# Where a query tile's low part, a rarely taken branch and a step's rows stand in a fused attention, experts and FFN kernel

## The chip, the cores and the metric

One core of a Trainium2 chip runs the whole program. The metric is the device time of one execution in microseconds (us). The engines are TensorE (PE), VectorE (DVE), ScalarE (ACT), GpSimd (POOL) and SyncE (SP); each takes its instructions in the order of the program, and they meet only at semaphores.

## What is computed

```python
def _attn_ref(q, k, v):                     # 4 x 8 heads, 576 rows, 64 columns
    scores = scale * np.matmul(q, k.transpose(0, 1, 3, 2))
    kth = np.partition(scores, -top_k, axis=-1)[..., -top_k:-top_k + 1]   # top_k = 32
    scores = np.where(scores >= kth, scores, -1000000000.0)
    attn = np.exp(scores - np.max(scores, axis=-1, keepdims=True))
    return np.matmul(attn / (np.sum(attn, axis=-1, keepdims=True) + 1e-09), v)

def _moe_ref(x, modality_id, w_gate, modality_bias, w1, w2):   # 2304 x 512, 8 experts, 1024
    logits = x @ w_gate + modality_bias[modality_id]
    e_idx = np.argmax(logits, axis=1)
...
    for e in range(E):
        h = np.maximum(x[mask] @ w1[e], 0.0)
        out[mask] = gate_w[mask, None] * (h @ w2[e])

def _moe2_ref(x, w_in, w_out):              # 2304 x 512, 2048
    h = x @ w_in
    g = np.where(h >= 1, h, np.where(h <= -1, 0.0, (h + 1) ** 2 / 4))
    return g @ w_out
```

## The kernel before

**Attention.** A pair is two heads of one batch; there are 16, each with 9 units of 128 queries. Two units are a group (72 groups), two groups share one tile of scores, a quad. The loop over groups `g` is written as a software pipeline: in the body of `g` the engines do the top 32 of group `g` (`topk`), the masks and transposes of group `g - 1`, the product with the values of group `g - 2`, and the scores of group `g + 4`.

`topk` on VectorE works on folded rows. In an odd group it also folds the next quad: `big` (L212), `c` (L213) and `lit2` (L214), the last two being the maximum and the minimum of the halves of `big`. GpSimd computes `lit`, the smaller one of each pair of scores (L227, L233: sum minus maximum), for the next group, and in an odd group waits with it until VectorE has made `lit2`. VectorE then takes the eight largest of `lit2` (L251) and of `lit` (L253). GpSimd also makes the small `nm` (L256) and the copies `edge` and `top` (L240), and for each pair `kl` and `ql` (L179, L183), which are the parts of keys and queries that the rounded `kh` and `qh` leave out, and the normalized output rows `x` and `xtail` (L348, L353).

Each pair is prepared some groups ahead: `turn` transposes keys or queries on TensorE and evicts them twice on ScalarE (`kT` and `kh`, `qT` and `qh`); `krest` and `qrest` make `kl` and `ql`. `prep` enters these four into the list `later` for the groups `g - 2` to `g`, where `g` is always odd. In its group such a list is worked off in order, its first two entries ahead of ScalarE's exponentials, the others at the body's end. `xout`, which makes `x` and `xtail` of an earlier pair, is put first in the list of an odd group.

**Experts.** Tokens are sorted by expert into chunks of 256 rows. A step is one or two chunks of an expert; for each of 8 columns `f` of its 1024 hidden units there is a piece `up` (L1054 to L1057, then `hh` and `hl`) and a piece `down` (L1063 to L1065). All pieces stand in one list, and `M.go(n)` writes out the next `n`. Ahead of each piece, `prepare` loads the weights of later pieces and splits those two pieces ahead into a high part (ScalarE) and a low part. The first two steps (`EARLY`) run while the routing of the last tokens is still being worked out: after each stage of `route_steps` on VectorE one piece is written out. The third step takes its expert and rows from the routing's table `tab`. In the second step `rows(st.next)` loads the third step's rows, and three of the later columns end with a `turn` that transposes them.

**The branch.** The top 32 of folded rows can miss an entry. `redo` says whether that happened anywhere; if so, a branch (L605) repeats the attention of that pair and `replay` repeats the experts' pieces done so far. Each engine reads `redo` and branches by itself; behind the branch the first use of another engine's work waits until that engine is through too. In the profiled run the branch's body isn't entered. Behind it, `reload` reads the registers of all steps that have some on SP again.

Of the kernel before, what the change touches and what calls it, by code (L numbers as in the profile page):

```python
# [23 lines left out]
NFE = FE // 128  # L24
# [6 lines left out]
EARLY = 2  # L31
# [34 lines left out]
class Kernel:  # L66
# [32 lines left out]
    def attention(self, moe):  # L99
        nc, tc = self.nc, self.tc  # L100
        with ExitStack() as ctx:
# [35 lines left out]
            raw, kq, st, xr = {}, {}, {}, {}  # L137
# [228 lines left out]
            def at(g, f, *a):  # L366
                later.setdefault(max(g, 0), []).append((f, a))

            def odd(g):
                return g if g % 2 else g - 1  # L370

            def prep(j, g, *eng):

                at(g - 2, turn, j, "k")
                at(g - 2, krest, j, *eng)
                at(g - 1, turn, j, "q")
                at(g, qrest, j, *eng)

            load(0, nc.scalar)
            load_v(0, vtile(0))  # L380
            load(1)
            load_v(1, vtile(1))
            prep(0, 0, nc.vector)
            for g in range(4):
                for f, a in later.pop(g, []):
# [5 lines left out]
            for j in range(1, len(pairs)):  # L391
                g = odd((9 * j + 1) // 2 - AHEAD - 2)
                prep(j, g)
                if j + 1 < len(pairs):
                    at(g - 2, load, j + 1)
# [150 lines left out]
            M = self.moe  # L546
# [35 lines left out]
            check_sum()  # L582
            for _ in self.route_steps():
                M.go(1)
            M.go(max(2 * NFE + 3 - M.at, 0))
            M.flush()
            M.apart = False

# [462 lines left out]
    def up(self, p, wh, wl, xh, xl, high=True, low=True):  # L1051
        nc = self.nc
        for c in range(KC if high else 0):
            nc.tensor.matmul(p, wh[c], xh[:, c, :], start=c == 0, stop=False)  # L1054
            nc.tensor.matmul(p, wl[c], xh[:, c, :], start=False, stop=False)  # L1055
        for c in range(KC if low else 0):
            nc.tensor.matmul(p, wh[c], xl[:, c, :], start=False, stop=c == KC - 1)  # L1057
# [221 lines left out]
class Experts:  # L1279
# [188 lines left out]
    def up(self, st, f):  # L1468
        nc = self.nc
        halves = st.next.halves if st.next else 0  # L1470
        if f == 2:
            self.rows(st.next)
        h, l = self.spl1.pop(self.n1[st, f])
        n = st.halves * 128
        p = self.bank("h")[:, 0:n]
        self.kn.up(p, [h[:, c] for c in range(KC)], [l[:, c] for c in range(KC)], st.xh, st.xl)
        hh, hl = (self.wide.tile([128, 2 * CAP], F32R, name="h" + x, bufs=2)[:, 0:n] if st.wide else
                  self.wk.tile([128, CAP], F32R, name="h" + x) for x in "hl")
        self.act(p, hh, hl)
        st.h[f] = hh, hl  # L1480
        t = f - NFE + 1 + halves
        if 0 <= t < halves:
            self.turn(st.next, t)
        if f == NFE - 2 and st.next and st.next.mate:
            self.rows(st.next.mate)
        self.work(self.up, st, f)
# [237 lines left out]
```

## Time and profile before

| | |
|---|---|
| median of 3 runs | 1181.84 us (1181.74 to 1182.97) |
| profiled execution | 1180.52 us, span 1178.9 us |
| busy: PE, DVE, ACT, POOL | 1109.3, 810.2, 709.8, 556.2 us |
| granted TensorE clock, mean | 0.977 |

The span is what the profile shows, from the first instruction to the last; the execution's own time is 1.6 us longer. Roughly, the attention takes the first 490 us, the experts run to 750 us, and the last network takes the rest. A busy time is the time in which an engine had an instruction under way; for TensorE, whose matmuls are pipelined, it is modelled.

### The profile page before, as it was taken

Reading aid. Unit: us, or ns where it says so; the run is one execution under the profiler, and the core shown is the slowest. Engines: PE = TensorE matmul, PEld = TensorE weight load, DVE = VectorE, ACT = ScalarE, POOL = GpSimd, SP = SyncE. Lnnn points to the kernel's source line nnn. Section 1 sums busy time; section 2 is a strip of 40 time slices with the busy share of each in tenths; the row PEclk is TensorE's granted clock in tenths of the full one; section 3 lists DMA queues with packets and bytes.
Section 4 is the critical chain, followed back from the end, with each engine's and each line's share of the span. In section 5 each row is a group of like instructions: output and inputs, shape, how many; then the busy total and the mean of one; then the engine's idle time right before and its main releaser. Section 6 shows DMA issues by size and latency. Waiting matters only on the chain. (4 is left out here: it accounts for less than half of the span.)

```text
span 1178.9 us, 24601 instructions
## 1 busy us (share of the span) xinstructions
PE 1109.3 (94%) x8900; PEld 944.4 (80%) x8901; DVE 810.2 (69%) x2523; ACT 709.8 (60%) x1262; POOL 556.2 (47%) x662
## 2 busy tenths in 40 slices
PE   8999899999998997887999999899999999999998
PEld 5777787877887885776888787778899999999897
DVE  6999999999999999887568889487332222323222
ACT  5989998999899985744554455254333333333322
POOL 2776777677677767622324455032322223232222
PEclk8989998999999997998999999999999999999999
DMA  4235573021111003366766565231101001010000
GB/s 88 55 114 176 185 233 119 15 45 44 25 27 37 12 13 126 108 205 212 239 198 214 187 224 179 78 130 54 54 1 37 19 1 54 1 55 1 27 1 28
DMA packets 120842, 106.66 MB, mean 90 GB/s; under 512 B 64384, under 2 KB 88960, under 8 KB 120704
## 3 DMA queue, kind: packets, MB, share of 16 engines
q1 hardware_dynamic: 116320, 94.67, 25.9%
q0 software_dynamic: 2880, 9.44, 2.4%
q8 instruction: 73, 1.20, 0.4%
q10 hardware_dynamic: 1504, 0.82, 0.2%
q14 instruction: 65, 0.53, 0.1%
HBM read 70.30 MB, written 34.60 MB: 89 GB/s over the span
## 5 line engine op out<-in xcount | busy, mean ns | idle before, releaser
L1206 POOL TENSOR_TENSOR gl<-g,gh 128x384 fp32r<-128x384 f32 x96 | 97.2, 1012 | 316.5 <-ACT gh L1205 289.5
L1200 ACT ACTIVATE c<-c,half 128x384 f32<-128x384 f32 x96 | 59.2, 617 | 161.9 <-DVE c L1199 157.1
L306 PE MATMUL tp<-nhuge,w 128*128 128x128 bf16 x720 | 137.1, 227 | 20.8 <-ACT w L295 20.5
L304 PE MATMUL tp<-ident,e 128*128 128x128 f32 x720 | 151.4, 297 | 0.5 <-issue 0.5
L1199 DVE TENSOR_SCALAR c<-h 128x384 f32<-128x384 f32 x95 | 52.8, 556 | 142.5 <-PE h L1057 140.1
L1054 PE MATMUL h<-xh,wih 128*128 128x384 f32 x380 | 130.5, 343 | 5.3 <-DVEq L1110 3.0
L1055 PE MATMUL h<-xh,wil 128*128 128x384 f32 x380 | 129.8, 341 | 0.0
L304 PEld LDWEIGHTS tp<-ident,e 128*128 128x128 f32 x720 | 105.4, 146 | 30.1 <-issue 11.2
L270 DVE MAX8 m<-z 128x8 f32<-128x160 f32 x432 | 117.5, 314 | 0.0
L1365 POOL TENSOR_TENSOR w1l<-w1r,w1h 128x512 fp32r<-128x512 f32 x41 | 57.7, 1408 | 124.7 <-ACT w1h L1364 98.4
L227 POOL TENSOR_TENSOR lit<-s 128x576 int32<-128x576 int32 x66 | 93.4, 1415 | 48.4 <-DVE lit L214 48.4
L1065 PE MATMUL y<-woh,gl 128*128 128x512 f32 x288 | 114.4, 397 | 1.5 <-POOL gl L1206 1.5
L1063 PE MATMUL y<-woh,gh 128*128 128x512 f32 x288 | 112.5, 391 | 1.7 <-ACT yo L1236 0.9
L1203 DVE TENSOR_TENSOR g<-c,h 128x384 f32<-128x384 f32 x95 | 52.6, 554 | 89.2 <-ACT c L1200 89.2
L1064 PE MATMUL y<-wol,gh 128*128 128x512 f32 x288 | 113.7, 395 | 0.0
L311 ACT ACTIVATE a<-tp 128x640 f32<-128x640 f32 x144 | 102.0, 708 | 18.9 <-PE tp L306 14.9
L295 ACT ACTIVATE w<-s,m 128x576 bf16<-128x576 f32 x144 | 103.6, 772 | 13.9 <-DVE m L270 13.9
L323 PE MATMUL tp<-v,a 128*64 128x65 f32 x2880 | 104.7, 228 | 2.1 <-issue 2.0
L323 PEld LDWEIGHTS tp<-v,a 128*64 128x64 f32 x2880 | 93.8, 141 | 15.5 <-issue 8.3
L290 ACT ACTIVATE e<-s,nm 128x576 f32<-128x576 f32 x144 | 103.5, 771 | 4.3 <-POOL nm L256 4.2
L306 PEld LDWEIGHTS <-w 128*128 128x128 bf16 x720 | 79.2, 111 | 26.9 <-ACT w L295 26.5
L204 ACT ACTIVATE s<-sp 128x576 f32<-128x576 f32 x144 | 92.8, 648 | 10.7 <-PE sp L196 9.1
(313 smaller groups left out, 2938.6 us busy)
## 6 DMA issues: line engine op xcount, KB each, us to landing
w1r<-in_moe_w_dram SPq DMA_DIRECT2D x56, 256.0 KB
w2r<-in_moe_w_dram SPq DMA_DIRECT2D x56, 256.0 KB
xs_dr<-zero SPq DMA_DIRECT2D x19, 512.0 KB
ys_dr<-zero SPq DMA_DIRECT2D x19, 512.0 KB
cr<-in_moe_w_in_dram SPq DMA_DIRECT2D x16, 512.0 KB
cr<-in_moe_w_out_dram SPq DMA_DIRECT2D x16, 512.0 KB
rows<-xs_dr SPq DMA_DIRECT2D x20, 256.0 KB
ys_dr<-rows SPq DMA_DIRECT2D x17, 256.0 KB
```

The costliest lines, as they stand in the source:

```text
L270: nc.vector.max(m8[:, i, r + 1], z[:, i])
L290: nc.scalar.activation(e, s, AF.Exp, bias=nm, scale=0.125)
L295: nc.scalar.activation(w, s, AF.Relu, bias=t, scale=-1.0)
L304: nc.tensor.matmul(o, e[:, k0:k0 + 128], self.ident, is_transpose=True, start=True, stop=False)
L306: nc.tensor.matmul(o, w[:, k0:k0 + 128], self.nhuge, start=False, stop=True)
L311: nc.scalar.activation(a, p[:, 0:640], AF.Relu)
L323: nc.tensor.matmul(o[HS[i]], a[:, k0:k0 + 64], v_[:, u % 2 if u < 8 else i, kc, :], start=kc == 0, stop=kc == 4)
L1054: nc.tensor.matmul(p, wh[c], xh[:, c, :], start=c == 0, stop=False)
L1055: nc.tensor.matmul(p, wl[c], xh[:, c, :], start=False, stop=False)
L1063: nc.tensor.matmul(y[t], hh[:, o], wh, start=first, stop=False)
L1064: nc.tensor.matmul(y[t], hh[:, o], wl, start=False, stop=False)
L1065: nc.tensor.matmul(y[t], hl[:, o], wh, start=False, stop=last)
```

## The change

```diff
             def prep(j, g, *eng):
...
                 at(g - 2, turn, j, "k")
                 at(g - 2, krest, j, *eng)
-                at(g - 1, turn, j, "q")
-                at(g, qrest, j, *eng)
+                at(g - 2, turn, j, "q")
+                at(g - 1, qrest, j, *eng)
...
             for _ in self.route_steps():
                 M.go(1)
-            M.go(max(2 * NFE + 3 - M.at, 0))
+            M.go(max(2 * NFE + 5 - M.at, 0))
             M.flush()
...
     def up(self, st, f):
         nc = self.nc
         halves = st.next.halves if st.next else 0
-        if f == 2:
+        late = st.n == EARLY - 1
+        if f == 2 + late:
             self.rows(st.next)
...
-        t = f - NFE + 1 + halves
+        t = f - NFE + 1 + halves - late
         if 0 <= t < halves:
             self.turn(st.next, t)
```

For each pair, the queries' transposes go from the even group `g - 1` to the end of the odd group `g - 2`, and `ql` from the odd group `g` to the even group `g - 1`. Two more pieces are written out ahead of the branch, `up` of column 2 and `down` of column 1 of the second step. In the second step the next step's rows are loaded at column 3 instead of 2, and transposed at columns 5 to 7 instead of 4 to 6.

On GpSimd, around one pair in the attention, from the keys' low part to the end of the odd group two later, the order before is:

```order
L179 TENSOR_TENSOR kl<-kT,kh 128x576
L240 COPY edge<-c 128x4
L240 COPY top<-m_1276 128x2
L256 TENSOR_SCALAR nm<-m_1410 128x2
L227 TENSOR_TENSOR lit<-s_1004 128x576
L233 TENSOR_TENSOR lit<-lit,big 128x576
L240 COPY edge<-c 128x4
...
L348 TENSOR_TENSOR x_73<-xr,r 128x4x128
L353 TENSOR_TENSOR xtail_77<-xr,r 64x64 x2
L183 TENSOR_TENSOR ql_116<-qT,qh_115 128x512
L240 COPY edge<-c 128x4
```

And after the change:

```order
L179 TENSOR_TENSOR kl<-kT,kh 128x576
L240 COPY edge<-c 128x4
L240 COPY top<-m_1276 128x2
L256 TENSOR_SCALAR nm<-m_1419 128x2
L227 TENSOR_TENSOR lit<-s_1013 128x576
L233 TENSOR_TENSOR lit<-lit,big 128x576
L183 TENSOR_TENSOR ql_116<-qT,qh_115 128x512
L240 COPY edge<-c 128x4
...
L348 TENSOR_TENSOR x_73<-xr,r 128x4x128
L353 TENSOR_TENSOR xtail_77<-xr,r 64x64 x2
L240 COPY edge<-c 128x4
```

`ql` has left its place behind `x` and `xtail` and stands behind the `lit` of the even group before them.

On SP, ahead of the branch, from the last transfer of the second step's pieces to the reading of `redo` (`tab` is the routing's table, `w1r` and `w2r` are raw weights), before:

```order
L1335 DMA w1r<-in_moe_w_dram 128x4x128
L1438 ISA
L1438 DMA ys_dr<-rows 128x512
L605 TENSOR_LOAD redo
L605 ISA x2
L605 COMPARE_AND_BRANCH
```

And after the change (lines are 1 or 2 higher there):

```order
L1439 DMA ys_dr<-rows 128x512
L1340 ISA
L1340 DMA w2r<-in_moe_w_dram 128x512
L1322 TENSOR_LOAD tab
L1322 ISA x2
L1319 TENSOR_LOAD tab
L1319 ISA x2
L1319 TENSOR_LOAD tab
L1319 ISA x2
L1336 ISA
L1336 DMA w1r<-in_moe_w_dram 128x4x128
L606 TENSOR_LOAD redo
```

Two loads of weights now come ahead of the branch, the second of them the third step's first, and with it three reads of that step's entries in the table.

## Rows read from the trace of the kernel before

**Rows 1.** Windows: length, busy PE, PEld, DVE, ACT, POOL, PEclk, DMA share, GB/s.
```profile
217.97:256.26 38.29, 35.97 (x500) 29.81 (x501) 36.71 (x156) 37.59 (x68) 27.04 (x36) 1.00 0.11 25
...
sum 349.58, PE 328.57 PEld 273.98 DVE 331.43 ACT 320.38 POOL 255.46; mean PE 27.38 PEld 22.83 DVE 27.62 ACT 26.70 POOL 21.29
...
750.00:1179.00 429.00, 415.54 (x2084) 371.41 (x2082) 155.91 (x270) 151.99 (x265) 112.66 (x111) 1.00 0.11 36
```

**Rows 2.** Groups from 50 to 440 us: busy us, mean ns, idle before, releaser.
```profile
L253 DVE MAX8 c<-lit 128x8 f32<-128x288 f32 x120 | 48.4, 445 | 18.1 <-POOL lit L233 18.1
...
L183 POOL TENSOR_TENSOR ql<-qT,qh 128x512 fp32r<-128x512 f32 x13 | 16.6, 1278 | 1.0
```

**Rows 3.** Timeline of GpSimd in an odd group: start, duration, instruction, idle before.
```profile
134.96 1.28 POOL L183 TENSOR_TENSOR ql<-qT,qh 128x512 fp32r<-128x512 f32 x1
136.18 0.19 POOL L240 COPY edge<-c 128x4 f32<-128x4 f32 x1
...
138.13 1.42 POOL L233 TENSOR_TENSOR lit<-lit,big 128x576 int32<-128x576 int32 x1
```

**Rows 4.** Timeline of VectorE, behind those rows and one quad later.
```profile
137.74 0.50 DVE L251 MAX8 c<-lit 128x8 f32<-128x144 f32 x2
139.59 0.82 DVE L253 MAX8 c<-lit 128x8 f32<-128x288 f32 x2 [1.34 <-POOL lit L233]
...
151.76 0.80 DVE L253 MAX8 c<-lit 128x8 f32<-128x288 f32 x2
...
152.93 1.34 DVE L212 TENSOR_TENSOR big<-s 128x1152 f32<-128x1152 f32 x1
```

**Rows 5.** Timeline of GpSimd at the end of an even group.
```profile
151.40 0.19 POOL L240 COPY edge<-c 128x4 f32<-128x4 f32 x1
...
153.10 1.24 POOL L256 TENSOR_SCALAR nm<-m 128x2 f32<-128x2 f32 x1 [1.39 <-DVE m L255]
```

**Rows 6.** Timelines of ScalarE and GpSimd in two pairs' preparation.
```profile
144.40 0.65 ACT L204 ACTIVATE s<-sp 128x576 f32<-128x576 f32 x1
146.58 1.44 ACT L295 ACTIVATE w<-s,m 128x576 bf16<-128x576 f32 x2 [1.53 <-DVE m L270]
...
151.68 0.59 ACT L172 ACTIVATE qh<-sp 128x512 fp32r<-128x512 f32 x1
...
236.15 0.65 ACT L175 ACTIVATE kh<-sp 128x576 fp32r<-128x576 f32 x1
...
237.12 1.44 POOL L179 TENSOR_TENSOR kl<-kT,kh 128x576 fp32r<-128x576 f32 x1
```

**Rows 7.** Timeline of TensorE around the branch.
```profile
530.24 0.29 PE L1054 MATMUL h<-xh,w1h 128*128 128x256 f32 x1
...
532.84 0.39 PE L1065 MATMUL y<-w2h,hl 128*128 128x512 f32 x1
537.10 0.39 PE L1054 MATMUL h<-xh,w1h 128*128 128x256 f32 x1 [3.87 <-ACTq L605]
539.97 0.58 PE L1055 MATMUL h<-xh,w1l 128*128 128x256 f32 x1 [2.49 <-DVEq L605]
...
548.99 0.60 PE L1045 MATMUL pT<-ident,rows 128*128 128x128 f32 x4
```

**Rows 8.** Timeline of VectorE around the branch.
```profile
532.59 0.42 DVE L1466 SCALAR_TENSOR_TENSOR hl<-h,hh 128x256 fp32r<-128x256 f32 x1
...
534.20 0.68 DVE L1365 TENSOR_TENSOR w1l<-w1r,w1h 128x512 fp32r<-128x512 f32 x1
...
535.99 0.15 DVE L945 CAST nsi<-ns 128x1 int32<-128x1 f32 x1
540.19 0.31 DVE L950 TENSOR_TENSOR lg<-lg,mx 128x144 f32<-128x144 f32 x1 [4.05 <-DVEq L605]
```

**Rows 9.** Timeline of SP's transfers behind the branch.
```profile
542.53 0.36 SPq L1339 DMA_DIRECT2D w2r<-in_moe_w_dram  x1
544.93 0.33 SPq L1380 DMA_DIRECT2D rows<-xs_dr  x1
```

## The prediction

> **What bounds the kernel now.** I read the table of windows first, cut at the moments where VectorE had just waited in the attention, then the groups of VectorE and GpSimd over the attention, then the timelines of the two engines around one such moment, and last the timelines around the branch.
>
> Twelve periods of the attention (75 to 425 us) last 349.58 us, in which VectorE is busy for 331.43, TensorE 328.57, ScalarE 320.38, GpSimd 255.46 [rows 1]. VectorE is first by a little, and its idle time has one cause: its maximum over `lit` (line 253) waits for GpSimd 18.1 us in all between 50 and 440 us; in the same stretch GpSimd makes `ql` 13 times [rows 2]. One of these waits: in an odd group GpSimd does `lit` for this group, the output rows `x` and `xtail`, then `ql` from 134.96, the copies from 136.18, and only then the `lit` of the next group, which ends at 139.55 [rows 3]. VectorE was through with line 251 at 138.24 and starts line 253 at 139.59, after 1.34 us of waiting; a group later it starts it at 151.76 without a wait [rows 4]. So `ql` stands ahead of the very result for which VectorE stops. The last 429 us belong to TensorE, busy for 415.54 [rows 1]: what is won earlier is carried to the end.
>
> **The change, part by part.**
>
> Low part of the queries. From the start of `ql` to the next instruction GpSimd spends 136.18 - 134.96 = 1.22 us [rows 3]. Without it the next `lit` ends at 138.33 instead of 139.55, against 138.24 on VectorE: of the wait of 1.34 some 0.1 stays. Over 13 pairs: 13 x 1.22 = 15.9 us of the 18.1 are taken away, 2.2 stay. All of this is on the path, as VectorE has no other idle time there to speak of.
>
> Where `ql` goes. It now follows the `lit` of the even group, ready at 151.40, where the copies start today; after them GpSimd waits 1.39 us for VectorE [rows 5]. So `ql` would run from 151.40 to about 152.6 and the two copies to about 152.9. VectorE's next fold begins at 152.93 [rows 4]. It costs nothing, but with hardly 0.1 us to spare. Without this cover it costs its 1.22 us again.
>
> The queries' transposes and their two evictions on ScalarE (`qh` 0.59 us, `qT` about the same) move from the body of the even group to the end of the odd one. There ScalarE is through at 145.05 and then waits 1.53 us for VectorE [rows 6]: about 1.1 us of evictions fits. `ql` finds its inputs at about 146.2, five us before GpSimd comes to it. The pair's loads are issued where they were, and nothing of the move issues a transfer.
>
> Can the others follow? TensorE and ScalarE have 21 and 29 us of idle time in the twelve periods, where VectorE gives up 12 x 1.22 = 14.6 [rows 1]. On average they can. In the period from 217.97 ScalarE is busy for 37.59 of 38.29 us [rows 1] and can't shorten it by 1.22; it will trail VectorE, which needs its scores only two groups later. The tight place is the keys' low part: `kh` ends at 236.80 and `kl` starts at 237.12 [rows 6]. With VectorE and GpSimd 1.22 us earlier and ScalarE not, `kl` waits 0.9 us, and about that goes to VectorE. I take 0.9 off, once: 15.0 us. The bounds: half, 8, if ScalarE or TensorE turn out to set the pace over long stretches (their busy shares are 92 and 94%), and 18.1, all of the wait.
>
> The branch. TensorE ends its last piece at 533.23, passes the branch in 3.87 us, starts one matmul, and waits 2.49 more until VectorE is through too, at 539.97 [rows 7]. VectorE came late: its last routing step ends at 536.14 and its first work behind the branch is at 540.19, 4.05 us later [rows 8]. The pieces that now come first, `up` 2 and `down` 1 of the second step, are 530.24 to 533.07 in length, 2.84 us for a pair [rows 7]. TensorE would reach the branch at 536.1, while VectorE first does three more instructions (`hl` 0.42, two weight splits of 0.68 [rows 8], some 1.6 us with their overlap) and passes at 541.5 or so. TensorE resumes 1.55 us later with 2.84 us more done: a gain of 1.3. It would be 2.8 if VectorE's three were hidden.
>
> The table's registers. SP now reads three of the table's values ahead of the branch, because the load of the third step's first weights is pulled ahead of it, and reads them again behind it. Three such reads take 544.93 - 542.53 - 0.36 = 2.0 us [rows 9]. Ahead of the branch they start when the table is ready (about 536) and delay SP to about 538.4. Behind it, the load of `w2r` and the three loads of rows queued behind the reads come about 2 us later, at 547 for the first rows. Their first transpose, now one column later in the step, stands 1.55 us later too, at about 550.5 instead of 548.99 [rows 7]. Of the present distance (4.1 us from issue to transpose) about 0.6 is lost, and no wait is visible there today. The last transpose now has one `down` (1.4 us) less until the third step uses the columns; two evictions of about 0.6 us fit. I cost this part at nothing; its bound is 3 us, if each of the three transposes waits about one us. The branch as a whole lies between -2 and +2.8 us.
>
> The sum: 15.0 + 1.3 = 16.3 us from the profiled execution's 1180.52, so 1164.2. The median of the runs is 1181.84, 1.3 above it: 1165.5 us.
>
> **A rule against it.** The `nm` that GpSimd starts at 153.10 lasts 1.24 us, until 154.34, just behind the end of VectorE's `big` at 154.27 [rows 4, 5]: of two that meet, one stands still. The Trainium skill, SBUF — State Buffer, section "SBUF: two separate sides", says that VectorE with two operands in SBUF and GpSimd share a port pair as an exclusive lock: whoever starts first keeps it for the whole instruction. By that rule a `ql` that is still running when the fold begins holds VectorE; the trace agrees for the other direction, and no row here shows this one.
>
> **The rivals.**
> - The moved `ql` meets the fold. If it runs some tenths late, as little as 0.1 to 0.3 us, VectorE's fold or GpSimd's copies wait. At worst the 1.22 us are paid there 13 times, 15.9 us are given back, and the branch's 1.3 is left: 1180.5, no change. For it: the gap ends at 152.93 and `ql` with its copies at 152.9. Against: copies and `nm` in VectorE's way are short, and the next `lit` waits for the fold anyway.
> - ScalarE or TensorE set the pace and half comes back: 1181.84 - 8 - 1.3 = 1172.5. For it: 37.59 of 38.29 us. Against: the spare time of the neighbouring periods.
> - The attention gives what it should, and the rows or the weights come late behind the branch, for 3 to 4 us: 1169.
> - Slower: GpSimd works in order, so if `qh` comes after GpSimd has reached `ql`, copies, `nm` and the next `lit` stand behind it. Today's figures leave 5 us (2.3 us in the tight period). If ScalarE trails VectorE by more than that, each further us lands on VectorE; from 1.22 us on, some 6.5 us of lag, it is worse than before. At 0.4 us beyond, 13 x 0.4 = 5 us: 1187. Against: ScalarE has less work than VectorE over the twelve periods.
>
> **How the numbers follow.** The forecast, 1165.5, has a chance of 0.70, the pace of the others 0.12, late rows 0.06, the fold 0.05, the slower case 0.04, and a gain above 18 us with a faster TensorE 0.03. The low end is all of the wait and all of the branch: 1181.84 - 18.1 - 2.8 = 1161. The high end takes in half of the attention's gain and a lost branch, 1174. Outside lie the fold, the slower case and the larger gain, 0.12, and the tails of the others: under 0.2 in all. A measurement of this kernel tells 0.2%, 2.4 us, from no change. Faster 0.91, the same 0.05, slower 0.04.
>
> **What would show it.** `ql` right behind the even group's second `lit`; line 253's waits for GpSimd down from 18.1 to 2 or 3 us, with no new wait at line 212; the attention's end 15 us earlier; the distance from TensorE's last matmul ahead of the branch to its second behind it down from 6.7 to about 5.4 us; the third step's transposes without a wait for their rows. Wrong would be: the waits at line 253 at the same sum, VectorE waiting for ScalarE's `s` or at line 212, or `kl` starting later than the `lit` ahead of it ends, in most pairs.

## The result, and the profile after

The changed kernel needs 1169.81 us in the median (1167.26 to 1177.03, 4 runs) where the kernel before needed 1182.40 beside it: ratio 0.9899, interval 0.9868 to 0.9930. A second reading, beside other kernels below, gave 0.9915 (0.9896 to 0.9934). By these numbers 10 to 12.6 us are gained. The forecast was 16.3 us and 1165.5. The profiled execution took 1170.9 us, with a span of 1169.3.

The windows again, first the same twelve periods of the attention (they answer to [rows 1]; length, busy PE, PEld, DVE, ACT, POOL, PEclk, DMA share, GB/s), then the end of the program.

```profile
74.33:411.99 337.66, 322.22 (x4169) 271.04 (x4166) 331.72 (x1401) 317.38 (x565) 256.50 (x331) 0.98 0.28 83
...
741.00:1169.00 428.00, 415.11 (x2083) 371.41 (x2081) 155.85 (x270) 151.88 (x265) 112.80 (x111) 1.00 0.11 36
```

VectorE has the same work, 331.7 us, in 337.66 instead of 349.58 us: its idle time went from 18.2 to 5.9. A period is 28.14 us long instead of 29.13. What lies ahead of them won another 0.95 (74.33 against 75.28), so that VectorE stands at line 253 at 411.99 where it stood at 424.86, 12.87 us earlier. The groups from 50 to 440 us show the same (busy us, mean ns, idle before, releaser; for [rows 2]):

```profile
L253 DVE MAX8 c<-lit 128x8 f32<-128x288 f32 x122 | 49.2, 445 | 4.7 <-POOL lit L233 4.1
...
L179 POOL TENSOR_TENSOR kl<-kT,kh 128x576 fp32r<-128x576 f32 x13 | 18.4, 1419 | 4.1 <-ACT kh L175 4.1
...
L183 POOL TENSOR_TENSOR ql<-qT,qh 128x512 fp32r<-128x512 f32 x13 | 16.7, 1283 | 0.0
```

Line 253 waits 4.1 us instead of 18.1. New against that profile is that `kl` waits for `kh`; in `branch_only` below, whose attention is the one before, it does so once, for 2.18 us. Now the timelines of GpSimd and VectorE at the end of an even group, the new place of `ql` (for [rows 4, 5]):

```profile
146.65 1.42 POOL L233 TENSOR_TENSOR lit<-lit,big 128x576 int32<-128x576 int32 x1
148.03 1.28 POOL L183 TENSOR_TENSOR ql<-qT,qh 128x512 fp32r<-128x512 f32 x1
149.25 0.18 POOL L240 COPY edge<-c 128x4 f32<-128x4 f32 x1
149.38 0.18 POOL L240 COPY top<-m 128x2 f32<-128x2 f32 x1
...
148.35 0.80 DVE L253 MAX8 c<-lit 128x8 f32<-128x288 f32 x2
...
149.52 1.34 DVE L212 TENSOR_TENSOR big<-s 128x1152 f32<-128x1152 f32 x1
```

`ql` ends at 149.31, its two copies at 149.56, and VectorE's fold starts at 149.52, without a wait and with its old length. In this pair that is the prediction's margin, to the tenth. In four of the 13 pairs between 50 and 440 us the fold begins 0.01 to 0.02 us ahead of `ql`'s end and takes 1.35 to 1.37 us, so there is nothing to spare. The waits that are left at line 253 are nine up to 411.99: seven of 0.19 to 0.30, and the two shown here, with the `kl` that stands ahead of each in GpSimd's timeline:

```profile
231.71 1.42 POOL L179 TENSOR_TENSOR kl<-kT,kh 128x576 fp32r<-128x576 f32 x1 [1.62 <-ACT kh L175]
...
307.83 1.42 POOL L179 TENSOR_TENSOR kl<-kT,kh 128x576 fp32r<-128x576 f32 x1 [1.84 <-ACT kh L175]
...
236.49 0.82 DVE L253 MAX8 c<-lit 128x8 f32<-128x288 f32 x2 [1.18 <-POOL lit L233]
...
312.57 0.82 DVE L253 MAX8 c<-lit 128x8 f32<-128x288 f32 x2 [1.37 <-POOL lit L233]
```

GpSimd stands 1.62 and 1.84 us at `kl`; five us later its `lit` is late for VectorE by 1.18 and 1.37.

At the branch, the timelines of TensorE, VectorE and of SP's transfers (for [rows 7 to 9]; line 606 is the branch):

```profile
523.35 0.39 PE L1066 MATMUL y<-w2h,hl 128*128 128x512 f32 x1
526.42 0.36 PE L1055 MATMUL h<-xh,w1h 128*128 128x256 f32 x1 [2.69 <-PEq L606]
527.50 0.52 PE L1056 MATMUL h<-xh,w1l 128*128 128x256 f32 x1 [0.72 <-DVEq L606]
...
538.84 0.66 PE L1046 MATMUL pT<-ident,rows 128*128 128x128 f32 x4 [2.61 <-DMA rows<-xs_dr]
...
524.59 0.68 DVE L1366 TENSOR_TENSOR w1l<-w1r,w1h 128x512 fp32r<-128x512 f32 x1
527.72 0.31 DVE L951 TENSOR_TENSOR lg<-lg,mx 128x144 f32<-128x144 f32 x1 [2.45 <-DVEq L606]
...
525.44 0.38 SPq L1336 DMA_DIRECT2D w1r<-in_moe_w_dram  x1
534.39 0.35 SPq L1340 DMA_DIRECT2D w2r<-in_moe_w_dram  x1
535.09 1.47 SPq L1381 DMA_DIRECT2D rows<-xs_dr  x3
```

From TensorE's last matmul ahead of the branch to its second one behind it there are 527.50 - 523.74 = 3.76 us; before there were 539.97 - 533.23 = 6.74. So the branch itself won 2.98 us. Eleven us on, the first transpose of the third step stands 2.61 us for its rows.

### The profile page after: what moved, and what is told of

The parts are those of the page before. It is cut to its first block, busy times and chain, and to the rows that moved or that the text cites. A ratio compares the mean times of both kernels' runs of the same rounds, so it can differ in the third digit from the quotient of the medians.

```text
span 1169.3 us, 24602 instructions
## 1 busy us (share of the span) xinstructions
PE 1106.4 (95%) x8900; PEld 944.4 (81%) x8901; DVE 807.9 (69%) x2524; ACT 708.7 (61%) x1262; POOL 553.9 (47%) x661
## 3 DMA queue, kind: packets, MB, share of 16 engines
q8 instruction: 74, 1.21, 0.4%
## 5 line engine op out<-in xcount | busy, mean ns | idle before, releaser
L304 PE MATMUL tp<-ident,e 128*128 128x128 f32 x720 | 144.8, 292 | 2.4 <-ACT e L290 2.4
L306 PE MATMUL tp<-nhuge,w 128*128 128x128 bf16 x720 | 133.2, 224 | 6.2 <-ACT w L295 5.1
L1366 POOL TENSOR_TENSOR w1l<-w1r,w1h 128x512 fp32r<-128x512 f32 x40 | 54.0, 1350 | 134.8 <-ACT w1h L1365 85.6
L311 ACT ACTIVATE a<-tp 128x640 f32<-128x640 f32 x144 | 102.3, 710 | 19.6 <-PE tp L306 15.2
L233 POOL TENSOR_TENSOR lit<-lit,big 128x576 int32<-128x576 int32 x66 | 93.5, 1417 | 5.2
```

What stands on the lines that cost most here:

```text
L304: nc.tensor.matmul(o, e[:, k0:k0 + 128], self.ident, is_transpose=True, start=True, stop=False)
L306: nc.tensor.matmul(o, w[:, k0:k0 + 128], self.nhuge, start=False, stop=True)
L311: nc.scalar.activation(a, p[:, 0:640], AF.Relu)
```

## The experiments

All kernels here were timed beside the kernel before, on the same chip; a ratio is to that kernel. They ran in three groups, each on another chip: `attn_only`, `branch_only`, `defer_load` and `rows_ahead`; `ql_twice`, `q_rest_only`, `k_first` and `defer_k_first`; and the other four. From one profile to the next the unchanged parts move by some us (below), so trace positions are compared over short distances and totals by ratios.

### The two parts apart

`attn_only` has the queries' part alone, `branch_only` the rest. Their edits against the changed kernel:

```diff
# attn_only
-            M.go(max(2 * NFE + 5 - M.at, 0))
+            M.go(max(2 * NFE + 3 - M.at, 0))
...
-        late = st.n == EARLY - 1
+        late = 0
# branch_only
-                at(g - 2, turn, j, "q")
-                at(g - 1, qrest, j, *eng)
+                at(g - 1, turn, j, "q")
+                at(g, qrest, j, *eng)
```

> Only the queries' part of the change; the branch and the third step's rows stand where they stood before. Theory A (the later branch wins some 2.8 us at the branch and gives them back until the FFN, because the rows and weights behind it come late): the attention's 12.9 us are all that the change was worth, so this kernel needs 1182.4 - 12.9 = 1169.5 us, no more than the changed kernel, and the third step's first transpose has no wait for its rows. Rival B (the later branch keeps its gain of 1.3 to 2.8 us, and the loss lies in the stages behind it whatever the branch does): 1169.8 + 1.3 to 1169.8 + 2.8, so 1171.1 to 1172.6 us.

> Only the branch two pieces later and the third step's rows one column later; the queries' part as before. Theory A: nothing is left of the gain at the branch, 1182.4 us within 1.5, with the wait of about 2.6 us for the rows at the third step's first transpose. Rival B (and the prediction's own term): 1.3 to 2.8 us faster, 1181.1 to 1179.6.

Measured: `attn_only` 0.9896 (0.9872 to 0.9920), `branch_only` 1.0007 (0.9987 to 1.0028). The queries' part alone is as good as the whole change, and of the branch's part no gain shows, within some 0.3%. The totals favour theory A but don't prove it: `attn_only`'s interval takes in the times of both theories, and `branch_only`'s still takes in, at its edge, a gain of 1.3 us (0.9989). In `attn_only` the third step's first transpose (535.77) has no wait, as theory A said. TensorE in `branch_only`, whose profiled execution (1190.22 us) was 5 us above its median:

```profile
544.55 0.55 PE L1055 MATMUL h<-xh,w1h 128*128 128x256 f32 x1 [2.75 <-PEq L606]
545.55 0.58 PE L1056 MATMUL h<-xh,w1l 128*128 128x256 f32 x1 [0.45 <-DVEq L606]
...
556.09 0.66 PE L1046 MATMUL pT<-ident,rows 128*128 128x128 f32 x4 [1.03 <-DMA rows<-xs_dr]
...
565.97 0.44 PE L1055 MATMUL h<-xh,w1h 128*128 128x384 f32 x1
```

The last row is the third step's first `up`. From the branch's second matmul to there it takes 20.42 us; in the kernel before 560.34 - 539.97 = 20.37, though there one more pair of pieces (2.84 us) lies between. So 2.89 us are given back in this stretch, against 2.98 won. Only 1.03 of them is the wait for rows; 0.67 is a wait for VectorE's `hl`. The rest has no row of its own (TensorE's clock stood at 0.50 for 5.1 us of this stretch, and for 4.4 before).

The other profiles say the same. From the end of VectorE's last routing step, `nsi`, to the third step's first `up` there are 24.2 us in the kernel before, 24.9 in `attn_only` and 24.2 in `attn_k_first` (below), which have its branch; in the seven profiles with the branch of the change, here and below, there are 24.2 to 25.3. What is won at the branch is gone at the third step in every one.

### What makes the rows late

Three ways to bring them earlier. `defer_load` holds the third step's first load, and with it the three table reads, until the branch is passed; `one_piece` passes the branch one piece later than before instead of two, where that load isn't due yet; `rows_ahead` issues the rows behind the branch ahead of everything but their three reads.

```diff
# defer_load, in load1; the held loads are issued after M.reload()
+            if self.hold is not None and st.e is None and st.n >= EARLY:
+                self.hold.append(k)
+                return
...
# one_piece
-            M.go(max(2 * NFE + 5 - M.at, 0))
+            M.go(max(2 * NFE + 4 - M.at, 0))
# rows_ahead
-            M.reload()
...
-        if f == 2 + late:
+        if f == 2 and not late:
...
+        one = self.steps[EARLY]
+        if one.e is not None:
+            self.regs(one)
+        self.rows(one)
+        for st in self.steps[:EARLY]:
+            self.regs(st)
```

> The changed kernel, but the load of the third step's first weights, with the three table reads that SyncE makes for it, is held back until SyncE is behind the branch. Theory 1 (the reads ahead of the branch keep SyncE at the branch and so make the rows late): SyncE passes the branch about 2 us earlier, the first rows are issued near 533 instead of 535.1, the wait of 2.61 us at the first transpose shrinks to 0.5 or so, and the kernel needs 1167 to 1168 us against 1169.8. Rival 2 (SyncE passes the branch when TensorE and VectorE do, and what makes the rows late is the seven reads and the weight load that stand ahead of them behind the branch, now one load more): the wait stays at 2.6 us or grows by 0.7, and the time stays at 1169.8 within 1.

> The changed kernel, but the branch comes one piece later than before instead of two. The load of the third step's first weights, with the table reads, then stands behind the branch by itself. If the table reads ahead of the branch are what makes the rows late, the wait for the rows at the third step's first transpose is 0.75 us or less, as in the run that holds this load back (2.61 in the changed kernel), and the third step's first up comes 1 to 2 us earlier against the last routing step. If it is the time from the branch to the rows' issue, whatever is read ahead, the wait is 2 us or more. Of the total 0 to 2 us below the changed kernel, which the interval hardly tells.

> The changed kernel, but behind the branch SyncE reads the third step's three registers first, then issues the three loads of rows, and only then reads the two early steps' four registers and loads w2r. Theory 1 and rival 2 of the run that holds the weight load back both say that the rows come some 3 us earlier and the wait of 2.61 us at the first transpose goes. Theory A goes on: as the rows were the loss, the kernel gains 2 to 2.6 us, 1167.2 to 1167.8. Rival C (w2r, now about 2 us later, is late next: ScalarE's w2h waits for it already, 2.71 us): TensorE waits for the second weights instead, and the time stays at 1169.8 within 1.

Measured: 0.9901 (0.9876 to 0.9925), 0.9903 (0.9875 to 0.9931) and 0.9900 (0.9878 to 0.9922). In the totals none differs from the changed kernel. The first transposes of `defer_load`, `one_piece` and `rows_ahead`:

```profile
537.70 0.66 PE L1048 MATMUL pT<-ident,rows 128*128 128x128 f32 x4 [0.75 <-DMA rows<-xs_dr]
```

```profile
543.27 0.60 PE L1046 MATMUL pT<-ident,rows 128*128 128x128 f32 x4
```

```profile
539.58 0.60 PE L1045 MATMUL pT<-ident,rows 128*128 128x128 f32 x4
...
544.78 0.66 PE L1045 MATMUL pT<-ident,rows 128*128 128x128 f32 x4 [1.62 <-DVE xl L1049]
...
542.43 0.63 ACT L1365 ACTIVATE w2h<-w2r 128x512 fp32r<-128x512 f32 x1 [4.58 <-DMA w2r<-in_moe_w_dram]
```

The wait for rows is not the same in each execution: in the seven profiles with the branch of the change it is 1.03 (`branch_only`) to 2.61 us, 2.16 in the changed kernel's second one. With the load held back it is 0.75, and nothing in `defer_k_first` (below); in `one_piece`, where TensorE also has a piece more to do ahead of the transposes, it is nothing too. So theory 1 holds for the wait: SP's reading of `redo` starts 2.1 us behind the end of the last routing step in the changed kernel, where it starts 3.0 us ahead of it in `defer_load` and `one_piece`, and 3.6 ahead in the kernel before. In `defer_load` the stretch from the end of VectorE's last routing step (524.44) to the third step's first `up` (546.20) is 21.76 us, where the changed kernel takes 24.36, from 523.72 to 548.08: 2.6 us less. In `defer_k_first` it is 22.4. So up to this point most of what the branch won is kept. The totals don't show it: the expected 1167 to 1168 us (0.987 to 0.988) lie at the lower edge of `defer_load`'s interval or below. In `rows_ahead` the rows come in time, but `w2r` is issued 10.9 us behind SP's last load ahead of the branch (528.79 to 539.71) instead of 8.95, ScalarE waits 4.58 us for it, VectorE's `w2l` and `xl` slip, and TensorE waits 1.62 us for `xl` at the second transposes instead: rival C. The rows were the first of several things that are late behind the branch.

### What the cover of `ql` is worth

`ql_twice` computes `ql` twice in a row; `q_rest_only` leaves the queries' transposes in the even group.

```diff
# ql_twice, in qrest
-                eng.tensor_tensor(lo, t[:, 0:512], hi.bitcast(F32), op=ALU.subtract)
+                for i in range(2):
+                    eng.tensor_tensor(lo, t[:, 0:512], hi.bitcast(F32), op=ALU.subtract)
# q_rest_only, in prep
-                at(g - 2, turn, j, "q")
+                at(g - 1, turn, j, "q")
```

> The changed kernel with ql computed twice in a row, at its new place behind the even group's second lit (same inputs, same output). It asks what the cover at the new place is worth: the first ql ends where VectorE's fold begins (237.62 against 237.68 in the changed kernel), so the second one runs into the fold. Theory 1 (the prediction's rival: of a ql and a fold that meet one stands still, and VectorE pays): the fold starts some 1.2 us later in 13 pairs, 1169.8 + 15.6, so about 1185 us, with idle time at lines 212 or 213 or a longer fold. Rival 2 (VectorE goes on; GpSimd, which waits 1.33 us for the fold's end before its next lit, takes the 1.2 us out of that wait): VectorE's waits at line 253 stay near 4 us and the time stays at 1169.8 within 2.

> The changed kernel, but the queries' transposes with qT and qh stay in the even group where they were, ahead of ql in the same group. ScalarE makes kh some 1.5 us after GpSimd is free for kl in the odd group; qh would come 2 to 3 us after GpSimd has reached ql in the even one. Theory 1 (the prediction's slower rival: copies, nm and the next lit stand behind a ql that waits, and what goes beyond the 1.33 us that GpSimd has to spare lands on VectorE): 13 times 0.3 to 1.4 us, so 1174 to 1188 us, with waits at line 253 or for the scores. Rival 2 (the wait takes the place of the one for the fold, and the lit of the odd group is needed only some 0.8 us after it is ready): within 2 us of 1169.8.

`ql_twice`: 1.0073 (1.0054 to 1.0091), some 20 us slower than the changed kernel and 8 slower than the kernel before. GpSimd and VectorE at one of its even groups, VectorE at another (212.11), and the fold's group from 50 to 440 us (line 213 there):

```profile
248.68 2.65 POOL L184 TENSOR_TENSOR ql<-qT,qh 128x512 fp32r<-128x512 f32 x2
...
250.19 2.35 DVE L213 TENSOR_TENSOR big<-s 128x1152 f32<-128x1152 f32 x1
...
212.11 1.34 DVE L213 TENSOR_TENSOR big<-s 128x1152 f32<-128x1152 f32 x1
213.48 1.72 DVE L214 TENSOR_TENSOR c<-big 128x576 f32<-128x576 f32 x1
...
L213 DVE TENSOR_TENSOR big<-s 128x1152 f32<-128x1152 f32 x30 | 50.3, 1677 | 0.0
```

The fold starts at 250.19, while the second `ql` runs until 251.33. It ends at 252.54, 1.21 us behind `ql`'s end where it needs 1.34 alone, and is recorded as 2.35 us of work, not as a wait. Ten of the 30 folds take 2.32 to 2.38 us, and all of them 50.3 instead of 30 x 1.343 = 40.3. In three pairs, such as that at 212.11, the fold starts first, by 0.1 us: then it keeps its 1.34 us, the second `ql` takes 2.4, and the next fold step stands instead (1.72 us). Line 254 (253 elsewhere) adds 4.1 us of waits, and the next fold step (0.855 instead of 0.760 us in the mean) 2.8. The named parts make 16.9 of the 20 us, and one more wait at line 254 ahead of 50 us another 2.8. Theory 1 holds, at more than its price. This is the rule that the prediction weighed (the Trainium skill, SBUF — State Buffer, section "SBUF: two separate sides": whoever starts first keeps the shared port for its whole instruction). The trace agrees: the fold advances only when `ql` is through, within 0.13 us, and where the fold is first it is `ql` that stands. So these two engines meet elsewhere than at semaphores, too.

`q_rest_only`: 0.9920 (0.9902 to 0.9938). GpSimd's `ql` from 50 to 440 us, VectorE's two long waits, and one `ql` with its fold:

```profile
L183 POOL TENSOR_TENSOR ql<-qT,qh 128x512 fp32r<-128x512 f32 x13 | 16.6, 1279 | 15.0 <-ACT qh L172 15.0
```

```profile
208.75 0.82 DVE L253 MAX8 c<-lit 128x8 f32<-128x288 f32 x2 [2.54 <-POOL lit L233]
...
325.13 0.82 DVE L253 MAX8 c<-lit 128x8 f32<-128x288 f32 x2 [2.68 <-POOL lit L233]
```

```profile
239.17 1.28 POOL L183 TENSOR_TENSOR ql<-qT,qh 128x512 fp32r<-128x512 f32 x1 [1.23 <-ACT qh L172]
...
239.39 2.27 DVE L212 TENSOR_TENSOR big<-s 128x1152 f32<-128x1152 f32 x1
```

GpSimd stands 15.0 us for `qh`, in five of the 13 pairs; in the other eight `qh` is in time. Twice it stands over 6 us, and VectorE waits 2.54 and 2.68 us for `lit`. Three times it stands 0.38 to 1.23 us, which puts `ql` into the fold, and VectorE pays as in `ql_twice`: the folds take 2.27, 1.85 and 1.42 us instead of 1.34, and one more ahead of 50 us takes 2.17. So theory 1 describes the pairs in which `qh` is late, by two ways that cost 5.2 and 2.3 us. Its attention ends at 477.79, 4.9 us later than the changed kernel's, of which the waits at line 253 make 2.7 and the folds 2.3; the ratios put the whole kernel 0.5 to 2.5 us behind the changed one. So the earlier transposes matter, and `ql` behind the even group's `lit` is worth having without them.

### Where the attention's last two us are

`k_first` puts the keys' transposes, `kT`, `kh` and `kl` ahead of the transposes and evictions `a` of the weights in the odd group. `defer_k_first` adds `defer_load`. Behind them came the changed kernel and `k_first` once more, side by side, and `attn_k_first`: the queries' part and the keys first, with the branch as before.

```diff
                     scores(g + AHEAD, 0)
+                if bg and bg[0][0] is turn and bg[0][1][1] == "k":
+                    for f, a in bg[:2]:
+                        f(*a)
+                    bg = [(id, (0,))] * 2 + bg[2:]
```

> The changed kernel, but in the odd group the keys' transposes, kT, kh and kl stand ahead of the transposes of the weights and their evictions a, which take ScalarE 1.46 us. Theory 1 (the attention gave 12.9 instead of 15.0 to 15.9 us because kl waited for kh, 6.9 us in five pairs, and VectorE lost 1.18 and 1.37 us by it): kl no longer waits, line 253's waits for GpSimd fall from 4.1 to about 1.5 us, the attention ends 2.5 us earlier, 1167.3 us. Rival 2 (ScalarE has no spare time in these periods; what kh gains, a and e lose, and the wait turns up at the scores or at the next nm): line 253 may fall, but VectorE's last line 253 stays at about 473 and the time at 1169.8 or above.

> Both mends together: the keys ahead of the weights' evictions as in the run before this one, and the third step's first weight load with its table reads held back behind the branch. If both theories hold, 2.5 us in the attention and 2.3 us between the branch and the third step's first rows: 1169.8 - 4.8 = 1165.0 us. If only the held load helps 1167.5; if neither, 1169.8.

> The changed kernel itself once more, beside the others of this job, so that differences of a few us between them can be read on one chip. Its ratio was 0.9899; if the reading repeats, 0.989 to 0.992. In its first profile the granted clock stood at 0.50 from 468 to 476 us, where the run with the keys first had 1.00; theory 1 (that level differs from execution to execution, whatever the kernel) says that the clock of this stretch is another one here.

> The kernel with the keys first once more. It came out 16.4 us faster than the kernel before, though its attention ended no earlier than the changed kernel's (472.7 against 472.9), and its lead showed only behind it, where the granted clock stood at 1.00 instead of 0.50. Theory 1 (the lead was the clock of these executions and the other chip): the ratio is that of the changed kernel beside it within 0.2%. Rival 2 (the order of ScalarE's work with the keys first keeps TensorE busier before the end of the attention, and the clock stays up more often): 0.3 to 0.4% below the changed kernel again, 0.986, with the clock at 1.00 between 468 and 480.

> The queries' part and the keys first, with the branch and the third step's rows where they were in the kernel before. If the later branch is worth nothing (its run alone gave 1.0007), this kernel equals the one with the keys first and the later branch, within 0.2%. If it is worth the prediction's 1.3 us or the 2.9 us that it wins at the branch itself, this kernel is 0.1 to 0.25% slower than that one.

Measured, with the sum of the waits above 0.5 us at line 253 up to 440 us, and how much earlier than before (485.79) VectorE's last line 253 stands. The last three rows are kernels of the sections above, whose attention is the changed kernel's:

| kernel | ratio, interval | long waits, us | earlier by, us | both, us |
|---|---|---|---|---|
| changed | 0.9899 (0.9868 to 0.9930) | 2.55 | 12.89 | 15.44 |
| after_again | 0.9915 (0.9896 to 0.9934) | 2.57 | 13.14 | 15.71 |
| attn_only | 0.9896 (0.9872 to 0.9920) | 1.83 | 13.35 | 15.18 |
| k_first | 0.9858 (0.9841 to 0.9875) | 1.79 | 13.08 | 14.87 |
| k_first_again | 0.9894 (0.9874 to 0.9914) | 1.06 | 14.76 | 15.82 |
| attn_k_first | 0.9876 (0.9851 to 0.9901) | 0 | 15.36 | 15.36 |
| defer_k_first | 0.9855 (0.9834 to 0.9876) | 2.31 | 13.16 | 15.47 |
| defer_load | 0.9901 (0.9876 to 0.9925) | 3.39 | 11.73 | 15.12 |
| rows_ahead | 0.9900 (0.9878 to 0.9922) | 6.24 | 9.12 | 15.36 |
| one_piece | 0.9903 (0.9875 to 0.9931) | 4.72 | 8.42 | 13.14 |

`attn_k_first` has none of these waits, and GpSimd's `kl` none for `kh` (groups of its attention):

```profile
L253 DVE MAX8 c<-lit 128x8 f32<-128x288 f32 x122 | 49.3, 446 | 2.1 <-POOL lit L233 1.5
```

```profile
L179 POOL TENSOR_TENSOR kl<-kT,kh 128x576 fp32r<-128x576 f32 x13 | 18.5, 1420 | 0.0
```

The last column is 15.4 within 0.6 in nine of the ten. In `one_piece` 2.2 us more are lost ahead of 60 us, in two of VectorE's instructions for the routing (1.53 and 1.42 us instead of 0.42 and 0.32). So the move of `ql` is worth some 15.4 us, and what `kl` loses by `kh` comes off it about one for one. The keys first don't reliably cure it: how many pairs wait, and which, differs between executions of one kernel. Still, the four profiles with the keys first lose 0 to 2.3 us by these waits, the six without 1.8 to 6.2, and all four ratios (0.9855 to 0.9894) lie below the six (0.9896 to 0.9915). Side by side the intervals overlap (0.9894 against 0.9915), so a gain of some 3 us is likely, and not shown. `attn_k_first`, without the later branch, is no slower than `k_first` (0.9876 against 0.9858 and 0.9894), and `defer_k_first` (0.9855) is level with `k_first` beside it (0.9858): no total shows a gain by the branch or by the held load.

`k_first`'s lead of its first reading was not in the attention: its last line 253 stands at 472.71, as rival 2 said, though the time that this rival gave (1169.8 or above) was missed by 4 us. In its profile TensorE started on the experts at 484.21, in the changed kernel's at 487.38, with the attention's end at the same place. The windows there, of the changed kernel and of `k_first` (columns as above, TensorE's clock third from the end):

```profile
464.00:468.00 4.00, 1.33 (x8) 0.95 (x9) 3.92 (x22) 3.04 (x5) 1.29 (x3) 0.77 0.51 182
468.00:472.00 4.00, 3.22 (x19) 2.43 (x17) 3.97 (x23) 2.01 (x3) 3.32 (x9) 0.50 0.70 199
```

```profile
464.00:468.00 4.00, 3.04 (x38) 2.07 (x39) 3.92 (x23) 3.20 (x6) 1.33 (x2) 1.00 0.51 171
468.00:472.00 4.00, 2.70 (x40) 2.10 (x39) 3.97 (x23) 3.24 (x7) 3.19 (x8) 1.00 0.62 197
```

The clock was at 0.50, the 1.2 GHz level, behind a stretch in which TensorE worked 1.33 of 4 us, and at 1.00, 2.4 GHz, where it had worked 3.04. In the second profile of the changed kernel this stretch had 1.00 again (theory 1 of that run), but the dip had come a little earlier, 0.50 from 455 to 465, and the experts still started at 487.03, so the level in this stretch alone does not settle when they start. `k_first_again` had 1.00 there, too, and its ratio was 0.21% below the changed kernel's beside it, which decides neither for its theory 1 (within 0.2%) nor for its rival 2 (0.986).

## Why the prediction was right, and where it was off

**What bounds the attention: right.** VectorE's idle time at line 253 was GpSimd's, and was on the path: without `ql` ahead of the `lit` VectorE has the same work in 11.9 us less over twelve periods.

**The low part of the queries: right in its mechanism, 2 us too large.** Forecast 15.0, in the trace 12.9, in `attn_only`'s time 12.3 (9.5 to 15.1). The step that failed is "I take 0.9 off, once". The place was right, `kl` behind `kh`; but it hit two pairs in each profile of the changed kernel, for 1.13 to 1.44 us each, 2.5 in all, and two or three pairs, 1.8 to 6.2 us, over the six profiles with this attention. `attn_k_first`, where it hits none, ends the attention 15.4 us earlier.

**The new place: right.** It "costs nothing, but with hardly 0.1 us to spare": `ql` and its copies end where the fold begins, and there is no wait at line 212. `ql_twice` shows what stood behind that margin, and that the rival of the fold was no empty one: once `ql` reaches into the fold the whole gain and 8 us more are gone.

**The slower rival** (`qh` late, GpSimd held) did not come about, since the transposes moved too. `q_rest_only` shows it in part: 15.0 us of waits for `qh`, of which 5.2 were passed on as waits and 2.3 as longer folds.

**The branch: two terms wrong, of opposite sign.** VectorE's three more instructions ended at 525.27, 1.55 us after its last routing step, as forecast (1.6). But it was behind the branch 2.45 us later, not 4.05, and so the branch won 2.98 us where the sum had 1.3. The sum put the passage behind the three instructions; it ran beside them. VectorE's reading of `redo`, by its sequencer, before and after (duration in ns, start in us):

```profile
L605 DVEq TENSOR_LOAD <-redo x1: 548/548/548, 536.0 to 536.0; - x1
```

```profile
L606 DVEq TENSOR_LOAD <-redo x1: 557/557/557, 523.9 to 523.9; - x1
```

Before, it starts 0.1 us ahead of the end of the last routing step; after, 1.4 us ahead of the end of the three instructions. From it to VectorE's next instruction there are 3.8 to 4.2 us in all 14 profiles. So the three were hidden, the case for which the prediction had 2.8.

**The rows "at nothing": wrong.** The step "no wait is visible there today" and "about 0.6 is lost" left out that a TensorE which resumes earlier also reaches the transposes earlier. The rows were issued nearly where forecast (the last routing step ends 12.4 us earlier than before; 12.4 us before the forecast's 547 is 534.6; it was 535.1) but landed 3.75 us later, 2.61 us too late. Of these 2.6 us 1.9 are TensorE's, which stood at the transposes at 536.23 instead of the forecast's 538.1; 0.5 are the later issue, and 0.2 that 3.5 us were left for the landing, where it took 3.75. The forecast's bound of 3 us held. The load and the table reads ahead of the branch are part of the cause: without them the wait was 0.75 us (`defer_load`) or none (`defer_k_first`), and the third step's first `up` came 2.6 us earlier after the routing. That the errors of the two terms leave so little between them is luck. Net the branch's part is 1.0007 (0.9987 to 1.0028), where a gain of 1.3 us, 0.9989, was the forecast; up to the third step's first `up` none is left (24.2 us from the last routing step in the kernel before, 24.4 in the changed one).

**The rest.** Of the 4 us that the forecast gave too much, 2.1 are the attention's and 1.3 the branch's; what is left is open. 12.9 from the attention and about nothing from the branch agree with the first reading (12.6 us by the medians, 11.9 by the ratio); the second, 10.1 us, is 2.8 less. The measured 1169.8 is also the number of the rival with late rows (1169), but that one had the attention give all that it should. From the third step's first `up` to the FFN's first matmul each profile of a kernel with the queries' part took 1 to 5 us longer than the kernel before's one profile (194.3 us; `attn_only` 198.4, `attn_k_first` 196.3, changed 197.6), and `branch_only` too (199.6). Part of that may be the choice of executions: the one profile before, of 1180.52 us, is below all the medians of that kernel here (1182.4 to 1185.2), and `branch_only`'s is 5 us above its own. In `attn_only` a later step's rows are waited for 2.68 us there, against 1.22 before, and the clock is 0.97 from 637 to 690 us; in `attn_k_first` that wait is 1.10. No one cause fits all, neither part of the change accounts for it, and it stays open.

## What to carry to other kernels

- Moving an instruction off the queue ahead of the result that the bounding engine waits for gives its full length each time (13 times 1.2 us here), if its new place lies in a gap and its own inputs come earlier too. Ask which other producer on that queue is now the last to be ready: here `kl`, which took two us or more back.
- A gap that fits to 0.1 us is good only while nothing in it grows. Doubling the moved instruction is a cheap way to see what lies behind.
- An engine that is let go earlier reaches the next transfer earlier. A load of which "no wait is visible today" has a margin; subtract the gain from it before it is costed at nothing.

## What the runs showed of the hardware that was not expected

A VectorE fold that met a running GpSimd subtraction was recorded as 2.35 us of busy time instead of 1.34, and not as a wait: such a loss is seen in the mean of a group (1677 against 1343 ns) and not in its idle column. `q_rest_only` has it too, 2.3 us in four folds. In the other direction the copy `top` of two numbers took 1.33 us instead of 0.19 where it fell into the fold (237.75 in the changed kernel), and cost nothing.

From VectorE's last line 253 to the experts' first matmul there are 11.5 us in `k_first`'s first profile and 13.7 in its second; over all kernels 11.5 to 15.2. Between 437 and 494 us TensorE's granted clock stood at 0.50, the 1.2 GHz level, for 10 to 31 us in each profile, in one or two stretches of 3.4 to 27 us at varying moments. A term of one or two us can't be read there from one profile.

VectorE's sequencer was at the branch, reading `redo`, while the engine still had 1.4 us of work to do; the 3.8 to 4.2 us from there to its next instruction hid that work.
